# A chunked delta-rule attention with a mixture of attention experts on one core: other PSUM pairs, other scratch, another written order

## The chip, the cores and the metric

One core of one Trainium2 chip runs the whole program, one launch. The metric is device time in microseconds (us) of one execution. Engines: PE (TensorE, matmuls), DVE (VectorE), ACT (ScalarE), POOL (GpSimd), SP (SyncE, which issues most DMAs). Each engine has its own queue and works it off in order.

## The reference

Two parts, one after the other. First, for each of 4 batches and 8 heads, a delta rule over 768 steps with a 48x48 state:

```
k_n = k / (norm(k) + 1e-6)
y[t] = q[t] @ state
state += beta[t] * outer(k_n[t], v[t] - k_n[t] @ state)
```

Then the heads are joined to `x` (4 x 768 x 384), and four experts of width 64 each do causal softmax attention on it:

```
q, k, v = x @ wq[e], x @ wk[e], x @ wv[e]
a = softmax(causal(q @ k.T / 8))
out += gate[e] * (a @ v @ wo[e])
```

The gate is a softmax over the two best of four logits `x @ w_gate`; the others are zero.

## The kernel before, in words

**Tiling.** The sequence is cut into 6 units (`n`) of 4 chunks (`c`) of 64 steps, 2 x 3 units over the batches. Within a chunk the recurrence is a triangular system: `gk` makes k'k products on PE, `ek` brings them to SBUF, `si` transposes 32x32 blocks so that a unit's blocks lie along the free dimension, `pre` gets norms and beta, `pa`, 31 steps `sv` and `pz` invert the triangular blocks by substitution (two tensor-tensor instructions a step, on DVE or POOL by the step's last argument), `so` and `sn` transpose back, and `ma`, eight copies `ea`, `mb`, eight copies `eb` join two 32-blocks to the inverse of 64.

Unit 0 takes another way, which is shorter: `ed` and `en` bring `gk` products to SBUF (`en` the whole masked product), fifteen steps `sb` invert blocks of 16 only, `so.0`/`sn.0` transpose back, and `zx`, `zp`, `ze` double them to 64 by five products a chunk (`zp.c.0` to `zp.c.4`) in four ring buffers for even and four for odd chunks (RING).

**State.** Per chunk: `ks` (k times state), `ex` (v minus it), `uu` (times the inverse), `eu`, `st` and `es` (new state), `yq` and `yu` (outputs, from `gq`/`eq` products and the state), `eh`/`el` (outputs as a high and a low part), and `hx` moves rows by DMA.

**Attention.** Per unit and half: projections `pj` (q and k) and `pv` (v and gate), split to high and low parts by `ph`/`pl`; row maxima `mx`/`em`/`mp`/`mr`/`er`; scores `sc`, exponentials `xp` on ACT, `av`, `oa`, normalising `nm`/`on`, and the output product `ft`, `fh`, `fl`, `fo`, `eo`, `do`. `gates` makes the gate's weights. `lw`, `wh`, `wl` load the weights and split them; `lk`, `lh`, `lv`, `lc`, `lz` load data and constants.

**Order.** Nothing is planned at run time. ORDER is a string of calls, `name.arguments:pair`, and the loop at the end of `tile_kernel` runs it word by word. An engine's queue is the words that issue on it, in that order. The number behind the colon is the PSUM pair (`PP`, 4 pairs of two banks) that the call writes or reads. An argument 0, 1 or 2 at the end of a name is the engine: ACT, DVE, POOL. `fill.n` is n small bf16 products that nothing reads.

In the lines: L182 is every matmul, L186 and L188 the copies of ACT and DVE, L342/L344 `ed`, L348 `en`, L356 `eq`, L360 `si`, L380 to L402 `pre`, L420/L422 `sv`, L425 `zt`, L429 `zm`, L436/L437 `sb`, L452 `sn`, L456 `so`, L302 `wl`, L410 `pz`, L471 `zx`, L619 `pl`, L763 `nm`.

Of the kernel before, what the change touches and what calls it, by code (L numbers as in the profile page):

```python
# [51 lines left out]
sv.1.4.1 eu.0.0.0:2 pre.1.7.1 sv.1.5.2 pre.1.6.1 wl.5.1 fill.3:0 yu.0.0:0 ze.2.0.0:1 zp.3.2:3 sv.1.6.2 eh.0.0.1:0
zp.3.3:3 ze.3.2.0:3 zp.2.1:1 sv.1.7.1 lw.2 ze.3.3.0:3 sv.1.8.2 el.0.0:0 fill.4:2 zp.3.4:2 ze.2.1.0:1 sv.1.9.2 st.0.0:3
lv.0.2 ze.3.4.0:2 gq.0.1:0 lv.0.3 es.0.0:3 gq.0.2:1 sv.1.10.2 wh.2.0 eq.0.1.1:0 wl.2.1 sv.1.11.2 fill.8:2 ks.0.1:2
eq.0.2.1:1 zp.2.2:3 sv.1.12.2 ex.0.1:2 yq.0.1:0 ze.2.2.0:3 uu.0.1:1 lk.2.1 sv.1.13.2 vt.0.2.1 fill.8:2 zp.2.3:3
vt.0.3.2 eu.0.1.0:1 yu.0.1:0 sv.1.14.2 ze.2.3.0:3 st.0.1:2 eh.0.1.0:0 gq.1.0:1 lv.1.0 el.0.1:0 sv.1.15.1 hx.0.0
es.0.1:2 fill.8:3 gq.0.3:3 sv.1.16.2 ks.0.2:0 eq.0.3.1:3 zp.2.4:2 sv.1.17.1 gk.2.0:3 ze.2.4.0:2 vt.1.0.1 sv.1.18.2
ex.0.2:0 eq.1.0.1:1 yq.0.2:2 vo ek.2.0.0:3 sv.1.19.1 gk.2.1:0 lk.2.2 uu.0.2:1 sv.1.20.1 ek.2.1.0:0 sv.1.21.1
pj.0.0.0:3 sv.1.22.1 eu.0.2.1:1 sv.1.23.1 yu.0.2:2 sv.1.24.1 ph.0.0.0.0:3 st.0.2:0 sv.1.25.1 pj.0.0.1:3 lv.1.1
sv.1.26.1 es.0.2:0 sv.1.27.2 eh.0.2.1:2 sv.1.28.2 pl.0.0.0:3 ks.0.3:1 sv.1.29.2 yq.0.3:0 ex.0.3:1 lk.2.3 sv.1.30.1  # L60
uu.0.3:1 vt.1.1.1 sv.1.31.2 eu.0.3.0:1 ph.0.0.1.1:3 st.0.3:1 pl.0.0.1:3 yu.0.3:0 pz.1.2 lv.1.2 es.0.3:1 gk.2.2:3
# [10 lines left out]
es.1.1:2 eg.0.1:0 yq.1.2:1 er.0.0.0:3 mp.0.1.2 sv.2.14.1 sc.0.0.0.0:2 sc.0.0.1.0:0 gates.0.1 xp.0.0.0.0:2 sv.2.15.2
ks.1.2:3 xp.0.0.1.0:0 av.0.0.0.0:2 lk.3.2 ex.1.2:3 sv.2.16.2 gates.0.0 lv.2.0 av.0.0.1.0:0 oa.0.0.0.1:2 mr.0.1:3
oa.0.0.1.0:0 sv.2.17.1 uu.1.2:2 er.0.1.0:3 pj.1.0.0:0 sv.2.18.1 eu.1.2.0:2 gates.0.2 sv.2.19.2 nm.0.0 st.1.2:3
sv.2.20.2 yu.1.2:1 lv.2.1 es.1.2:3 gk.3.2:2 eh.1.2.0:1 ph.1.0.0.1:0 gq.2.1:3 sv.2.21.2 ek.3.2.0:2 pj.1.0.1:0
pl.1.0.0:0 eq.2.1.1:3 on.0.0.2 sv.2.22.1 pv.1.0:3 el.1.2:1 sv.2.23.2 ph.1.0.1.1:0 sv.2.24.2 pl.1.0.1:0 mx.1.1.0.0:2
# [5 lines left out]
fill.8:3 ft.0.1:3 es.1.3:1 eo.0.0.0:2 ma.2:0 pre.3.0.1 fh.0.1.0:3 do.0.0 pj.1.1.0:1 sn.2 pre.3.1.2 vt.2.2.2 fl.0.1:3
pv.1.1:2 ea.2.0.1.1.0:0 ea.2.1.0.1.0:0 ea.2.1.0.0.1:0 ea.2.1.1.1.0:0 pre.3.2.1 ph.1.1.0.0:1 pre.3.3.2 ea.2.0.0.0.0:0
pl.1.1.0:1 pj.1.1.1:1 ea.2.1.1.0.0:0 eg.1.1:2 ea.2.0.0.1.0:0 gates.1.0 pre.3.4.1 ea.2.0.1.0.0:0 gates.1.1 pre.3.5.2
ev.1.1.0:2 pa.3.2 ks.2.0:3 ph.1.1.1.0:1 mb.2:0 ex.2.0:3 pl.1.1.1:1 mx.1.1.1.1:2 eb.2.0.1.1.0:0 eb.2.0.0.0.1:0
mx.1.0.0.1:3 sv.3.1.2 eb.2.0.0.1.0:0 fo.0.1.0:1 em.1.1.1.1:2 eb.2.1.1.0.0:0 sv.3.2.2 eb.2.0.1.0.0:0 eb.2.1.1.1.0:0
pre.3.7.2 eb.2.1.0.0.1:0 yq.2.0:2 eb.2.1.0.1.0:0 sv.3.3.1 uu.2.0:0 lk.4.0 sv.3.4.1 fo.0.1.1:1 eu.2.0.0:0 em.1.0.0.1:3
sv.3.5.2 yu.2.0:2 eo.0.1.0:1 sv.3.6.1 gq.2.3:0 gates.1.2 sv.3.7.2 st.2.0:3 eh.2.0.0:2 do.0.1 mx.1.1.0.1:1 lv.2.3
eq.2.3.0:0 el.2.0:2 es.2.0:3 gk.4.0:2 em.1.1.0.1:1 ks.2.1:3 ek.4.0.0:2 sv.3.8.2 yq.2.1:0 ex.2.1:3 lk.4.1 mx.1.0.1.1:1
uu.2.1:3 sv.3.9.1 sv.3.10.1 sv.3.11.1 eu.2.1.0:3 vt.2.3.2 fill.8:2 yu.2.1:0 em.1.0.1.1:1 st.2.1:2 sv.3.12.2 eh.2.1.0:0  # L90
gq.3.0:3 lv.3.0 lk.5.0 el.2.1:0 gk.4.1:1 eq.3.0.1:3 mp.1.0.2 hx.2.0 es.2.1:2 sv.3.13.2 mr.1.0:0 ks.2.2:3 er.1.0.0:0
mp.1.1.1 ek.4.1.0:1 sc.1.0.0.1:2 sv.3.14.2 ex.2.2:3 fill.2:0 mr.1.1:0 xp.1.0.0.1:2 yq.2.2:1 pre.3.6.1 vt.3.0.1
uu.2.2:3 er.1.1.0:0 lk.4.2 sv.3.15.2 sc.1.0.1.0:2 eu.2.2.1:3 yu.2.2:1 sv.3.16.1 xp.1.0.1.0:2 gq.3.1:0 sv.3.17.2
pj.2.0.0:3 eh.2.2.0:1 eq.3.1.1:0 el.2.2:1 sv.3.18.1 pv.2.0:2 sv.3.19.1 ph.2.0.0.0:3 sv.3.20.1 sv.3.21.1 gk.4.2:0
ev.2.0.0:2 eg.2.0:2 sv.3.22.2 pl.2.0.0:3 mx.2.0.1.0:1 ek.4.2.0:0 mx.2.1.0.0:2 pj.2.0.1:3 em.2.0.1.0:1 sv.3.23.1
em.2.1.0.0:2 sv.3.24.2 av.1.0.1.0:0 ph.2.0.1.0:3 sv.3.25.2 pl.2.0.1:3 mx.2.1.1.0:1 st.2.2:2 em.2.1.1.0:1 sc.1.0.0.0:3
lv.3.1 sv.3.26.2 es.2.2:2 sc.1.1.0.1:1 xp.1.0.0.0:3 sv.3.27.1 ks.2.3:2 sv.3.28.1 xp.1.1.0.1:1 yq.2.3:3 sv.3.29.1
sv.3.30.1 lk.4.3 av.1.0.0.0:1 ex.2.3:2 sv.3.31.2 lv.3.2 av.1.0.0.1:1 vt.3.1.2 pz.3.1 uu.2.3:2 oa.1.0.0.0:1
sc.1.1.0.0:1 eu.2.3.0:2 yu.2.3:3 so.3 xp.1.1.0.0:1 gk.4.3:2 eh.2.3.0:3 av.1.1.0.0:1 ek.4.3.0:2 el.2.3:3 av.1.1.0.1:1
vt.3.2.1 hx.2.1 sc.1.1.1.1:3 sc1.3.0.0 si.4 sc.1.0.1.1:2 xp.1.1.1.1:3 xp.1.0.1.1:2 gq.3.2:3 oa.1.1.0.1:1 pre.4.0.1  # L100
# [780 lines left out]
```

## Time and profile before

| | us |
|---|---|
| median of 3 runs | 451.3 (451.19 to 453.36) |
| profiled execution, its own time | 452.6 |
| its span | 450.9 |
| mean granted PE clock in it | 0.964 |
| PE busy | 392.5 |
| DVE busy | 313.7 |
| ACT busy | 182.0 |
| POOL busy | 171.3 |

The span is from the first to the last instruction of the profiled execution; the 1.7 us around it are start and end of the launch. Busy times are sums over the span, so they average over stages with different limits; a stretch of its own tells more. A wait is put down to what ended it last. [...]

### The profile page before, as it was taken

Reading aid. Unit: us, or ns where it says so; the run is one execution under the profiler, and the core shown is the slowest. Engines: PE = TensorE matmul, PEld = TensorE weight load, DVE = VectorE, ACT = ScalarE, POOL = GpSimd, SP = SyncE. Lnnn points to the kernel's source line nnn. Section 1 sums busy time; section 2 is a strip of 40 time slices with the busy share of each in tenths; the row PEclk is TensorE's granted clock in tenths of the full one; section 3 lists DMA queues with packets and bytes.
Section 4 is the critical chain, followed back from the end, with each engine's and each line's share of the span. In section 5 each row is a group of like instructions: output and inputs, shape, how many; then the busy total and the mean of one; then the engine's idle time right before and its main releaser. Section 6 shows DMA issues by size and latency. Waiting matters only on the chain.

```text
span 450.9 us, 22827 instructions
## 1 busy us (share of the span) xinstructions
PE 392.5 (87%) x10407; PEld 352.6 (78%) x10407; DVE 313.7 (70%) x655; ACT 182.0 (40%) x349; POOL 171.3 (38%) x314
## 2 busy tenths in 40 slices
...
GB/s 187 242 101 17 45 136 85 124 3 75 90 36 45 84 106 124 42 109 20 1 40 132 137 58 1 3 39 40 92 73 82 61 5 10 12 4 38 38 3 70
DMA packets 15441, 29.43 MB, mean 65 GB/s; under 512 B 2801, under 2 KB 8945, under 8 KB 15345
## 3 DMA queue, kind: packets, MB, share of 16 engines
...
q10 hardware_dynamic: 256, 0.39, 0.3%
q14 instruction: 16, 0.12, 0.1%
...
## 4 chain that ended last, share of the span: by engine, by line
PE 67%; DVE 16%; DMA 6%; ACT 5%; issue 4%; POOL 1%; SPq 0%; DVEq 0%; ACTq 0%
PE ps L182 67%; DMA kq<-in_kq_dram 6%; DVE tn L452 2%; ACT tt L186 1%; ACT bl L186 1%; DVE ql L619 1%; DVE xh L590 1%; DVE mx L684 1%; DVE bl L360 1%; DVE tt L190 1%; DVE pm L356 1%; ACT qh L186 1%; DVE tn L436 1%; DVE sb L562 1%; DVE gc L653 1%
## 5 line engine op out<-in xcount | busy, mean ns | idle before, releaser
L422 POOL TENSOR_TENSOR tp<-bl 128x238 f32<-128x238 f32 (+13 forms) x90 | 44.7, 497 | 75.0 <-DVE bl L420 59.2
L743 ACT ACTIVATE at<-ps 128x768 f32<-128x768 f32 (+1 forms) x48 | 43.8, 919 | 40.9 <-PE ps L182 40.7
L182 PE MATMUL ps<-kq 48*64 48x64 f32 x1536 | 38.2, 241 | 16.5 <-issue 5.2
L684 DVE TENSOR_REDUCE mx<-ps 128x2 f32<-128x1024 f32 (+3 forms) x48 | 44.8, 952 | 9.6 <-PE ps L182 9.3
L420 POOL TENSOR_TENSOR bl<-bl,tp 128x238 f32<-128x238 f32 (+13 forms) x90 | 46.6, 518 | 7.1
L182 PEld LDWEIGHTS ps<-kq 48*64 48x64 f32 x1536 | 32.2, 152 | 20.9 <-issue 11.3
L182 PE MATMUL ps<-xh,wqkh 128*128 128x256 f32 x288 | 44.7, 291 | 1.2 <-DVE ql L619 0.9
L182 PE MATMUL ps<-vs,at 128*64 128x65 f32 x1344 | 45.2, 224 | 0.0
L182 PEld LDWEIGHTS ps<-vs,at 128*64 128x64 f32 x1344 | 41.4, 138 | 2.9 <-issue 0.8
L182 PEld LDWEIGHTS ps<-xh,wqkh 128*128 128x128 f32 x288 | 37.9, 191 | 3.1 <-DVE ql L619 1.6
L186 ACT ACTIVATE tt<-ps 32x256 f32<-32x256 f32 (+2 forms) x87 | 33.4, 384 | 15.7 <-PE ps L182 9.6
L182 PE MATMUL ps<-qh,kh 64*128 64x256 f32 x192 | 35.2, 362 | 0.0
L182 PE MATMUL ps<-kh,qh 64*128 64x512 f32 (+3 forms) x128 | 26.3, 435 | 3.6 <-DVE kl L619 1.9
L182 PE MATMUL ps<-ql,kh 64*128 64x256 f32 x192 | 28.1, 289 | 0.0
L182 PE MATMUL ps<-qh,kl 64*128 64x256 f32 x192 | 28.1, 288 | 0.0
L182 PEld LDWEIGHTS <-ide 64*128 64x128 bf16 (+1 forms) x479 | 23.1, 103 | 6.1 <-issue 1.4
L182 PE MATMUL ps<-mr,sel 64*128 64x256 bf16 x192 | 27.4, 281 | 0.0
L182 PE MATMUL ps<-mask,ide 64*128 64x128 bf16 (+1 forms) x384 | 26.1, 217 | 0.0
L182 PE MATMUL ps<-wvgh,xh 128*128 128x260 f32 x144 | 24.8, 297 | 1.4 <-DVE pm L356 1.4
L182 PE MATMUL ps<-xh,wqkl 128*128 128x256 f32 x144 | 24.9, 282 | 0.0
L422 DVE TENSOR_TENSOR tp<-bl 128x210 f32<-128x210 f32 (+14 forms) x60 | 21.4, 357 | 3.0 <-POOL bl L420 2.1
L420 DVE TENSOR_TENSOR bl<-bl,tp 128x210 f32<-128x210 f32 (+14 forms) x60 | 21.6, 360 | 2.1
...
## 6 DMA issues: line engine op xcount, KB each, us to landing
...
kq<-in_kq_dram SPq DMA_DIRECT2D x12, 96.0 KB, 4.2
...
kq<-in_kq_dram ACTq DMA_DIRECT2D x4, 96.0 KB, 3.8
...
```

The costliest lines, as they stand in the source:

```text
L182: T.matmul(o, lhsT=a, rhs=b, start=start, stop=stop, skip_group_check=True)
L186: S.activation(o, x, AF.Copy, **({} if scale is None else {"scale": scale}))
L190: V.tensor_scalar(o, x, scale, None, op0=OP.mult)
L356: (V if e else G).tensor_tensor(t, P if e else t, pmask[:, None, None, :].to_broadcast([128, 2, 4, 64]), op=OP.mult)
L360: V.transpose(BB[n % 2], d.rearrange("p t j -> p j t"))
L420: e.tensor_tensor(X[:, a:b, i + 1:], X[:, a:b, i + 1:], tv, op=OP.subtract)
L422: e.tensor_tensor(tv, R[:, :, i + 1:].to_broadcast([128, w, m]), X[:, a:b, i:i + 1].to_broadcast([128, w, m]), op=OP.mult)
L436: E.tensor_tensor(tv, BD[:, :, i:i + 1, i + 1:].to_broadcast([128, 2, i, m]), BD[:, :, 0:i, i:i + 1].to_broadcast([128, 2, i, m]), op=OP.mult)
L452: V.transpose(TN[n % 2].rearrange("p t l -> p l t"), BB[n % 2])
L562: V.tensor_tensor(s[0:112], s[0:112], ax(k)[0:112], op=OP.add)
L684: V.tensor_reduce(d, two(k)[:, :, a:a + 128 * (k1 - k0)], axis=AX.X, op=OP.max)
L743: S.activation(at_of(n, b, y, kp)[:, :, 0:w], two(k)[:, :, 0:w], AF.Exp, scale=0.125)
```

## The change

Four things. (1) `pj.n.h.0` and `pj.n.h.1`, the q and k projections of a half, wrote the two banks of one pair and now write two different pairs. (2) The ring buffers of odd chunks in unit 0 were `KV[2]`, `PM[1]`, `PM[2]` and `AT[2]`; now they are two parts of `KF` that held `ed`'s result, and two parts of `BX[0]`, the matrix of unit 0's substitution. (3) `en` gets an engine: 1 is the product on DVE out of PSUM as before, 0 a copy on ACT and the product on POOL in place; all four are 0 now. All fifteen `sb` are on DVE (1 to 6 were on POOL). (4) All of ORDER is another: the same calls, each once, in another order, with other engines and pairs, 18 `fill` words (132 products) instead of 16 (95). 55 steps of `sv` go from DVE to POOL and 17 the other way; on POOL are then 133 of 155. Of the 40 `ea` and 40 `eb`, 17 and 15 are on DVE instead of 8 and 10; `on` 8 of 12 instead of 3; `eq` 10 of 24 instead of 16; `eu` 4 of 24 instead of 9; `wl` 1 of 7 instead of 6.

The diff, cut: the start of ORDER, the part around `ma.1` and `mb.1`, and the code.

```diff
-lh.0.1.0.1 zg lc.0 lz lh.0.0.0.0 lh.0.3.0.1 lh.0.2.0.0 lk.1.2 init lk.1.0 lw.0 lc.1 lw.3 lk.1.1 fill.8:0 gk.0.1:0
-ed.1:0 lc.2 gk.0.0:1 lk.1.3 ed.0:1 gk.0.3:2 lv.0.0 ed.3:2 lh.0.3.1.0 gk.0.2:3 ed.2:3 lh.0.1.1.0 lh.0.0.1.0 si.0 lw.1
-lw.5 lh.0.2.1.0 pre.0.0.1 zm lv.0.1 wh.0.0 en.3:2 pre.0.1.2 en.0:1 gk.1.0:2 wh.3.0 pre.0.2.1 gk.1.2:1 ek.1.0.0:2
-pre.0.3.1 wl.3.1 zt pre.0.4.1 cb gk.1.1:2 en.1:0 pre.0.5.2 ek.1.1.0:2 lw.4 pre.0.7.1 gk.1.3:0 ek.1.2.1:1 sb.1.2
-ek.1.3.0:0 sb.2.2 sb.3.2 en.2:3 sb.4.2 si.1 sb.5.2 gq.0.0:2 sb.6.2 lk.2.0 eq.0.0.1:2 wh.1.0 sb.7.1 wh.5.0 sb.8.1
-sb.9.1 sb.10.1 sb.11.1 sb.12.1 sb.13.1 sb.14.1 wh.4.0 sb.15.1 wl.4.2 so.0 sn.0 zx.1.0.0 zx.0.0.0 fill.8:1 zp.1.0:1
-zp.1.1:1 pre.1.0.1 ze.1.0.0:1 zx.1.1.0 zp.0.0:0 pre.1.1.1 wl.1.1 ze.1.1.0:1 zp.0.1:0 pre.0.6.1 ze.0.0.0:0 wl.0.1
...
-eq.1.1.0:2 si.2 yq.1.0:3 sc1.1.0.0 gq.1.2:0 sc1.1.1.0 lk.3.0 pre.2.0.1 eq.1.2.0:0 ma.1:2 ev.0.0.1:1 eg.0.0:1 sn.1
-pj.0.1.0:1 pre.2.1.2 ea.1.0.1.0.1:2 ea.1.1.1.1.0:2 pre.2.2.1 ea.1.1.0.0.0:2 pj.0.1.1:1 pre.2.3.1 ea.1.1.1.0.0:2
-ea.1.0.0.0.0:2 pre.2.6.1 ea.1.0.0.1.0:2 pre.2.4.1 ea.1.0.1.1.0:2 pre.2.5.1 pa.2.1 pre.2.7.2 ea.1.1.0.1.0:2
-ph.0.1.0.0:1 mb.1:2 ph.0.1.1.0:1 pl.0.1.0:1 sv.2.1.2 mx.0.1.1.0:0 eb.1.1.0.1.0:2 eb.1.0.0.0.1:2 sv.2.2.2
-eb.1.0.0.1.0:2 eb.1.1.0.0.1:2 sv.2.3.2 eb.1.0.1.1.0:2 pl.0.1.1:1 eb.1.1.1.0.0:2 eb.1.1.1.1.1:2 eb.1.0.1.0.0:2
...
+lz lc.0 lh.0.3.0.1 fill.22:0 gk.0.3:0 lh.0.1.0.1 lh.0.2.0.0 ed.3:0 fill.1:1 gk.0.1:1 ed.1:1 gk.0.2:2 ed.2:2 lh.0.0.0.0
+gk.0.0:3 ed.0:3 si.0 init lk.1.2 pre.0.0.1 pre.0.1.1 pre.0.2.1 lc.2 lh.0.3.1.0 pre.0.3.1 pre.0.4.1 lw.2 en.1.0:1
+en.2.0:2 zm lh.0.0.1.0 lh.0.2.1.0 pre.0.6.1 lk.1.0 lc.1 pre.0.5.1 en.3.0:0 zt pre.0.7.1 gk.1.2:1 ek.1.2.0:1 cb sb.1.1
+sb.2.1 sb.3.1 gk.1.0:2 lw.0 wh.2.0 lw.3 gq.0.2:1 sb.4.1 sb.5.1 en.0.0:3 eq.0.2.0:1 sb.6.1 lv.0.1 sb.7.1 lh.0.1.1.0
+lk.1.1 sb.8.1 zg wh.3.0 lk.1.3 fill.28:0 gk.1.1:0 wh.0.0 sb.9.1 sb.10.1 sb.11.1 sb.12.1 sb.13.1 sb.14.1 sb.15.1 wl.0.2
+wl.2.2 lw.4 lv.0.2 lw.5 wl.3.2 so.0 fill.5:3 gk.1.3:3 lw.1 lv.0.0 ek.1.0.0:2 ek.1.1.0:0 vt.0.1.2 wh.4.0 ek.1.3.0:3
+gq.0.1:1 eq.0.1.0:1 gq.0.0:2 sn.0 zx.0.0.0 zx.1.0.0 fill.15:0 zp.0.0:0 lw.6 zp.0.1:0 wh.1.0 si.1 pre.1.0.1 zx.0.1.0
+wl.4.2 vt.0.2.2 wh.6.1 ze.0.1.0:0 zp.1.0:3 ze.0.0.0:0 pre.1.1.2 zx.1.1.0 zp.1.1:3 ze.1.1.1:3 wl.6.1 lk.2.0 pre.1.2.1
+pre.1.3.2 zp.0.2:1 wl.1.2 wh.5.0 zp.0.3:1 ze.1.0.0:3 ze.0.3.0:1 ze.0.2.0:1 zp.1.2:0 zp.1.3:0 pre.1.4.1 pre.1.5.2
+zp.0.4:3 eq.0.0.1:2 ze.1.3.0:0 ze.1.2.0:0 ze.0.4.0:3 vt.0.0.2 fill.4:1 uu.0.0:1 zx.2.0.0 eu.0.0.0:1 pa.1.1 pre.1.6.1
...
+ek.2.0.1:3 ev.0.0.1:0 gk.2.3:2 ks.1.0:1 gq.1.2:3 eg.0.0:0 pj.0.0.0:0 pz.1.2 ek.2.3.0:2 eq.1.2.0:3 so.1 si.2 pre.2.0.1
+sc1.1.1.0 sc1.1.0.0 pre.2.1.2 ph.0.0.0.0:0 ex.1.0:1 pl.0.0.0:0 pre.2.2.1 pj.0.0.1:2 ma.1:3 sn.1 vt.1.2.2 pre.2.3.2
+pre.2.4.1 ea.1.0.1.0.1:3 gq.1.1:1 eq.1.1.0:1 pre.2.5.2 ea.1.0.1.1.1:3 pa.2.2 sv.2.1.2 sv.2.2.2 sv.2.3.2 ea.1.1.1.0.1:3
+ea.1.1.0.0.0:3 pre.2.6.1 sv.2.4.2 sv.2.5.2 pv.0.1:0 ea.1.0.0.1.0:3 ph.0.0.1.0:2 pj.0.1.1:1 ea.1.1.0.1.0:3
+ea.1.1.1.1.0:3 ea.1.0.0.0.0:3 ph.0.1.1.0:1 mb.1:3 eg.0.1:0 gates.0.0 sv.2.6.2 sv.2.7.2 eb.1.0.1.1.0:3 pl.0.0.1:2
+sv.2.8.2 sv.2.9.2 ev.0.1.1:0 pre.2.7.1 eb.1.1.0.0.0:3 eb.1.0.0.1.0:3 eb.1.0.1.0.0:3 eb.1.1.1.0.0:3 pj.0.1.0:2
+ph.0.1.0.0:2 eb.1.1.0.1.1:3 eb.1.1.1.1.1:3 yq.1.0:0 eb.1.0.0.0.1:3 pl.0.1.1:1 uu.1.0:3 mx.0.0.0.0:1 lk.3.0 pl.0.1.0:2
...
@@ -343,10 +343,12 @@
         for a in range(2):
             V.scalar_tensor_tensor(d[:, a], P[:, a, :, 0:32], hm[:, 0:1], d[:, a], op0=OP.mult, op1=OP.add)
 
-    def en(c, k):
+    def en(c, e, k):
         P = two(k)[:, :, 0:256].rearrange("p a (b i) -> p a b i", b=4)
-        V.tensor_tensor(TG[0][:, NP * c:NP * c + NP].rearrange("p (a b) i -> p a b i", a=2), P,
-                        nmask[:, None, None, :].to_broadcast([128, 2, 4, 64]), op=OP.mult)
+        t = TG[0][:, NP * c:NP * c + NP].rearrange("p (a b) i -> p a b i", a=2)
+        if not e:
+            S.activation(t, P, AF.Copy)
+        (V if e else G).tensor_tensor(t, P if e else t, nmask[:, None, None, :].to_broadcast([128, 2, 4, 64]), op=OP.mult)
 
     def eq(n, c, e, k):
         P = two(k)[:, :, 0:256].rearrange("p a (b i) -> p a b i", b=4)
@@ -367,7 +369,7 @@
     fl_ = lambda t: t.rearrange("p a b c -> p (a b c)")
     RING = [[x[:, 0:512].rearrange("p (a b) -> p a b", b=64) for x in r] for r in (
         (KF[:, 2432:], fl_(ON), fl_(OS[0]), fl_(OS[1])),
-        (fl_(KV[2]), PM[1].rearrange("p a b -> p (a b)"), PM[2].rearrange("p a b -> p (a b)"), AT[2][:, 0]))]
+        (KF, KF[:, 512:], flat(BX[0]), flat(BX[0])[:, 512:]))]
     BD = BX[0].rearrange("p a b -> p (a b)").rearrange("p (k r) -> p k r", k=2)[:, :, 0:512].rearrange("p k (a b) -> p k a b", b=32)[:, :, :, 0:16]
 
     def pre(n, k, e):
```

## Rows read from the trace of the kernel before

**Rows 1.** Which engine is busy how long, from the page's first part

```profile
PE 392.5 (87%) x10407; PEld 352.6 (78%) x10407; DVE 313.7 (70%) x655; ACT 182.0 (40%) x349; POOL 171.3 (38%) x314
```

**Rows 2.** Stretches: length; PE, PEld, DVE, ACT, POOL busy; PE clock, DMA share, GB/s

```profile
0.00:33.00 33.00, 13.77 (x304) 11.39 (x304) 23.41 (x51) 12.04 (x29) 10.08 (x27) 1.00 0.72 181
...
100.00:373.00 273.00, 249.02 (x6798) 223.08 (x6790) 203.84 (x431) 114.36 (x221) 120.26 (x211) 0.95 0.22 62
373.00:442.00 69.00, 68.24 (x1360) 61.62 (x1360) 31.50 (x65) 25.24 (x34) 6.58 (x18) 0.98 0.07 22
```

**Rows 3.** What PE waited for, 40 to 374 us: total, times, longest

```profile
PE ps L182 <- issue: 12.4, 13, 1.7
PE ps L182 <- DVE kl L619: 2.5, 2, 1.9
...
PE ps L182 <- DVE os L188: 0.4, 1, 0.4
```

**Rows 4.** Busy time by stretch, the six half-rate stretches: first, and sum

```profile
97.70:104.50 6.80, 5.89 (x150) 5.17 (x153) 4.41 (x11) 1.79 (x4) 4.57 (x10) 0.50 0.09 18
...
sum 30.60, PE 29.59 PEld 25.67 DVE 19.04 ACT 7.35 POOL 12.83; mean PE 4.93 PEld 4.28 DVE 3.17 ACT 1.23 POOL 2.14
```

**Rows 5.** Timeline of DVE in the first unit: start, us, line, operation

```profile
18.22 0.67 DVE L400 TENSOR_TENSOR bl<-bl,aa 128x512 f32<-128x512 f32 x1
...
25.50 0.27 DVE L436 TENSOR_TENSOR tn<-bl 128x108 f32<-128x108 f32 x1
...
28.31 0.63 DVE L436 TENSOR_TENSOR tn<-bl 128x28 f32<-128x28 f32 x1
28.98 0.21 DVE L437 TENSOR_TENSOR bl<-bl,tn 128x28 f32<-128x28 f32 x1
...
30.18 1.91 DVE L456 STREAM_TRANSPOSE vs<-bl 128x1024 f32<-128x1024 f32 x1
...
139.97 1.72 DVE L763 TENSOR_TENSOR rsm<-gt,rsm 128x8 f32<-128x8 f32 x1
```

**Rows 6.** Timeline of POOL, the same stretches

```profile
12.54 0.60 POOL L429 MEMSET bl<- 128x256 f32 x2 [9.46 <-DVE bl L360]
...
15.34 1.28 POOL L425 TENSOR_TENSOR bl<-bl,vs 128x512 f32<-128x512 f32 x1 [0.71 <-DVE rr L386]
...
28.09 0.79 POOL L302 TENSOR_TENSOR wvgl<-at,wvgh 128x268 fp32r<-128x268 f32 x1 [4.32 <-ACT wvgh L186]
...
139.76 1.91 POOL L410 TENSOR_TENSOR bl<-bl,na 128x1024 f32<-128x1024 f32 x1
```

**Rows 7.** Timeline of ACT, the start

```profile
2.65 1.28 ACT L284 ACT_TABLE_LOAD   x1 [2.65 <-issue]
...
9.42 0.47 ACT L342 ACTIVATE vs<-ps,cst 128x256 f32<-128x256 f32 x1 [0.38 <-PE ps L182]
...
36.62 0.60 ACT L186 ACTIVATE pm<-ps 128x512 f32<-128x512 f32 x1 [2.80 <-PE ps L182]
```

**Rows 8.** Timeline of PE, the first zp groups and one gq

```profile
33.08 1.97 PE L182 MATMUL ps<-tt,kv 64*64 64x64 f32 x32 [8.47 <-ACT kv L471]
34.84 1.73 PE L182 MATMUL ps<-kv,tt 64*64 64x64 f32 x32
36.41 1.10 PE L182 MATMUL ps<-tt,vs 64*64 64x64 f32 x32
...
64.53 0.69 PE L182 MATMUL ps<-kq 48*64 48x64 f32 x32
```

**Rows 9.** The chain that ended last: start, us, what; one projection half

```profile
359.42 2.41 PE ps L182 x18
```

**Rows 10.** Groups of instructions, one of the two of an sv step

```profile
L422 POOL TENSOR_TENSOR tp<-bl 128x238 f32<-128x238 f32 (+13 forms) x90 | 44.7, 497 | 75.0 <-DVE bl L420 59.2 <-DVE rsm L761 6.1 <-DVE gw L657 5.3
L422 DVE TENSOR_TENSOR tp<-bl 128x210 f32<-128x210 f32 (+14 forms) x60 | 21.4, 357 | 3.0 <-POOL bl L420 2.1
```

**Rows 11.** DMA issues by line, 0 to 60 us: KB each, us to landing

```profile
bta<-in_beta_dram SPq DMA_DIRECT2D x1, 96.0 KB, 7.0
```

More of the change, by code (lines that the diff above doesn't have):

```diff
@@ L52 @@
[L52 to L61, printed above, removed]
@@ L72 @@
[L72 to L76, printed above, removed]
@@ L82 @@
[L82 to L100, printed above, removed]
-mx.2.0.0.0:1 sc1.3.1.0 av.1.0.1.1:0 eq.3.2.1:3 ma.3:2 em.2.0.0.0:1 oa.1.0.1.0:0 sc.1.1.1.0:3 nm.1.0 sn.3 on.1.0.2
```

190 lines of the change are left out of this document (110 added, 80 removed).

## The prediction

> **What bounds the kernel now.** I read the page's totals first. TensorE (PE) is busy 87% of the span, VectorE (DVE) 70%, POOL 38% [rows 1]: PE is the engine to ask about, DVE the one that can hold it. The table of stretches comes next [rows 2]. In the first 33 us PE works 13.8 us, while the DMA engines are 72% busy: that stretch is loading and the first unit's substitution. From 100 to 373 PE works 249.0 of 273 us, and from 373 to 442 it has 68.2 of 69: the last stretch has no stall to win. So an order can win in two places, at the start and in the stalls up to 373.
>
> What ends those stalls is in the table of waits of PE [rows 3]. From 40 to 374 us, 12.4 us in 13 pieces are ended by nothing that the profile shows; the same number of instructions is issued after the change, so I leave them. Twelve lines of DVE, the first 2.5 and the last 0.4, add up to 14.8 us; ACT, POOL and DMA have 5.5. [...]
>
> The sum is made against the profiled execution's own time, 452.6 us (span 450.9 and 1.7 around it), which lies 1.3 above the median of 451.3.
>
> **The start, up to so.0.** `pre.0.7` needs `zt`, which now stands on POOL behind `en.1`, `en.2`, `zm` and `en.3`. The new `en` is a copy on ACT (0.60, by the copy of one PSUM tile at 36.62) and a product on POOL of the size of `zt` (1.28) [rows 6, 7]. `init` and its table load (1.28) now follow the last `ed` on ACT, which ends at 9.89 [rows 7]: the first copy ends at 11.8, and POOL then needs four times 1.28 and 0.6 for `zm` [rows 6], until 17.5. `pre.0.7` (0.67) ends at 18.2; before it ended at 18.89 [rows 5]. Beta is 672 KB later in SP's queue (2699 KB ahead of it instead of 2027). Before it landed 7.0 us behind an issue at about 7.1; at 181 GB/s that is 3.7 us more [rows 2, 11], 17.8, some 0.3 behind `zt`; I take nothing for it, 0.6 if DMA is slower than its mean.
>
> Then all fifteen `sb` run on DVE. Steps 9 to 14 take 3.3 us without the held one (25.50 to 28.31, and twice 0.25); steps 1 to 6 have the same widths, and 7 and 8 cost 0.62 each: 7.8 us. With 0.96 for `sb.15` and 1.91 for `so.0`, `so.0` ends at 28.9 instead of 32.1 [rows 5]: -3.2 at best.
>
> But POOL was nearly idle under DVE's steps, and no longer is. In the one case that overlapped, POOL's `wl.4` ran 28.09 to 28.88 and a DVE step of 0.21 took 0.63, to 28.94; and a DVE product of eight columns took 1.72 until POOL's 1.91 was over [rows 5, 6]. [...] The new order has six POOL operations there (`en.0`, `eq.0.2`, `wl.0`, `wl.2` at 1.28, `wl.3` and `vt.0.1` at 0.79): 6.7 us, less the step of 0.25 that each lets through, +5.2 over the best. The ten operations of `pre` that can be held meet POOL as well: up to 2.5 more. The ends are -3.2 and +4.5; I take +1.0, nearer to the held one, as the rows show it.
>
> [...]
>
> **The start, on PE.** The 32 records of `zp.1.0` and `zp.1.1` took 1.97 and 1.73, the third such group 1.10 [rows 8]: PE came out of idling at the lower level. Now 28, 5 and 15 fills precede `zp.0.0` instead of 8 that ended 8.5 us earlier, so I count 1.97 + 1.73 - 2.2 = -1.5 (0 if PE idles long again). `gq.0.1` and `gq.0.2` move ahead of `zp`, into idle time: two of some 0.5 (32 records in 0.69, the next group beginning before the end) [rows 8], -1.0. The new ring buffers are dead by then, except that `ze.1.0` now writes the matrix that `sn.0` still reads: `sn.0` ends 1.9 behind `so.0`, under three `zp` of 1.1, so nothing; 1.9 if that cover goes.
>
> **Unit 1's entry (ma.1 to uu.1.0).** The longest DVE-ended stall, 1.9 of PE on `kl` [rows 3], is here, followed at once by the first half-rate stretch, 6.8 us [rows 4]. Now `gq.1.1`, `pv.0.1` and `pj.0.1.1` lie behind `ma.1` and `pj.0.1.0` behind `mb.1`: three products of 2.4 [rows 9] where two lay. -1.9 for the stall, and -1.7 for half of the 3.4 that the clock can give back: -3.6 (0 to -5.3).
>
> **DVE against POOL from there on.** 38 steps of `sv` go from DVE to POOL, two instructions each, 0.36 on DVE and 0.50 on POOL [rows 10]: 27 us less on DVE, 38 more on POOL. Five `on` (0.7) and 14 copies of `ea` and `eb` (0.4) come to DVE, 9 us, and `en`, `eq`, `eu` and `wl` leave it for about as much: it falls to some 290 us. All of it lies beside PE's work; it pays only where a DVE line ends a stall. Of the 14.8 less the 1.9 above I take -1.0 (0 to -12.9): a new order also makes new stalls.
>
> **A pair for each projection.** A projection takes 2.41 [rows 9]; two halves held one pair, now each has its own until its copies are done. Nothing shows four pairs under such use. PE's waits for `kl`, 2.5 [rows 3], can go, or as much can come where another matmul waits for a pair: -2.5 to +2.5, and I take 0, since the 1.9 is counted already.
>
> **Fills.** 95 become 132, but behind `zp.0.0` and before the last eight groups 63 become 45. Eight warm ones are some 0.8: 18 fewer are at most -1.8; most stood in stalls, so -0.5.
>
> Sum: +1.0 - 1.5 - 1.0 - 3.6 - 1.0 + 0 - 0.5 = -6.6. 452.6 becomes 446.0, and on the median's scale 444.7: I say **445 us**. About 0.5% is what a measurement here can tell from no change: under 449.0 counts as faster, over 453.6 as slower.
>
> **Rivals.**
> *POOL holds DVE (slower).* [...] Price: +4.5 instead of +1.0 at the start; unit 1's chain is then late, so 3.6 and the 1.0 of relief are not gained, and holds in later `gates` and `nm` add some 1.5: 445 + 3.5 + 3.6 + 1.0 + 1.5 = 455. It decides from `so.0` ending after about 36. For it: the held rows. [...]
> *Stalls move (same).* PE stays bound by its queue, and each stall that goes returns elsewhere. Only the start's terms remain, -1.5: 450.
> *The clock stays up (faster).* The stalls that precede half-rate stretches go. [...] For it: PE's cover is better at unit 1. Against it: five of the six stretches lie where I see no edit aimed at them.
> [...]
> *The change doesn't do what it says* would be projections whose halves still wait for each other; it prices as the second rival.
>
> **Chances.** Forecast 0.48 (own range 440 to 449), stalls move 0.20, POOL holds DVE 0.20, clock 0.12. Faster than 449.0: nearly all of the first and last, a few of the second, 0.60; same 0.20; slower 0.20. The range reaches half way into the clock case and just over the hold: 437 to 456.
>
> **What would show it.** In the changed profile: `so.0` ending near 33 (29 without holds, over 36 with all), and `sb` steps beside POOL operations longer than 0.3; the first `zp` at 1.1; no stall of over 1 us before `uu.1.0` and the clock whole from 97 to 105; DVE's busy time near 290 and POOL's near 215; PE's DVE-ended waits under 13 us. The prediction is wrong if `zp.0.0` starts after 38, or if half-rate time exceeds 31 us.

## The result, and the profile after

| | median us | lowest to highest | runs |
|---|---|---|---|
| before | 452.27 | 446.16 to 457.24 | 20 |
| after | 446.23 | 442.36 to 449.58 | 20 |

The ratio is 0.990, with a 95% interval of 0.9865 to 0.9928: the kernel after is 1.0% faster. The prediction was 445 us, 1.4% under the 451.3 known then. The profiled execution of after took 449.6 us (span 447.9), the highest of its 20 and one of four in a slower state, which the ratio leaves out, so the two traces differ by only 3.0 us where the medians differ by 6.0. The trace of e5, the same kernel once more at 446.9 us (span 445.2), is set beside it where that matters.

The page's first part, against [rows 1]:

```profile
PE 391.5 (87%) x10444; PEld 356.2 (80%) x10444; DVE 301.2 (67%) x598; ACT 180.8 (40%) x344; POOL 219.8 (49%) x381
```

DVE lost 12.5 us and POOL gained 48.5; PE is as busy as it was. The stretches, with the columns of [rows 2]:

```profile
0.00:33.00 33.00, 18.40 (x423) 15.87 (x423) 24.12 (x50) 14.61 (x35) 17.97 (x22) 0.80 0.79 206
100.00:373.00 273.00, 248.48 (x6968) 225.36 (x6972) 195.32 (x381) 116.64 (x223) 163.30 (x290) 0.95 0.22 63
```

In the first 33 us POOL works 18.0 us instead of 10.1. What that did to DVE stands in two timelines of after, DVE first, then POOL (start, us, line, operation; L438 and L439 are the two instructions of a step `sb`, lines being two higher than before; a POOL row of x2 is two operations in a row):

```profile
22.21 0.25 DVE L438 TENSOR_TENSOR tn<-bl 128x88 f32<-128x88 f32 x1
22.49 1.20 DVE L439 TENSOR_TENSOR bl<-bl,tn 128x88 f32<-128x88 f32 x1
23.72 1.23 DVE L438 TENSOR_TENSOR tn<-bl 128x100 f32<-128x100 f32 x1
...
27.07 1.21 DVE L439 TENSOR_TENSOR bl<-bl,tn 128x108 f32<-128x108 f32 x1
28.32 0.72 DVE L438 TENSOR_TENSOR tn<-bl 128x112 f32<-128x112 f32 x1
29.08 0.78 DVE L439 TENSOR_TENSOR bl<-bl,tn 128x112 f32<-128x112 f32 x1
29.89 0.27 DVE L438 TENSOR_TENSOR tn<-bl 128x112 f32<-128x112 f32 x1
...
34.75 1.91 DVE L458 STREAM_TRANSPOSE vs<-bl 128x1024 f32<-128x1024 f32 x1
```

```profile
22.21 2.62 POOL L302 TENSOR_TENSOR wqkl<-at,wqkh 128x512 fp32r<-128x512 f32 x2
24.79 1.31 POOL L302 TENSOR_TENSOR wvgl<-at,wvgh 128x512 fp32r<-128x512 f32 x1
26.05 0.86 POOL L531 TENSOR_TENSOR kv<-kv,nt 128x384 f32<-128x384 f32 x1
26.88 1.28 POOL L358 TENSOR_TENSOR pm<-pm,cst 128x512 f32<-128x512 f32 x1
28.12 0.79 POOL L302 TENSOR_TENSOR wvgl<-at,wvgh 128x268 fp32r<-128x268 f32 x1
28.88 0.85 POOL L531 TENSOR_TENSOR kv<-kv,nt 128x384 f32<-128x384 f32 x1
```

Seven POOL operations stand back to back from 22.21 to 29.73, and seven DVE instructions each end some 0.1 us behind one of them: DVE got one instruction in for each of POOL's. While POOL is idle the same DVE instruction takes 0.27. `so.0` ends at 36.66; before it was 32.09 [rows 5].

PE's waits over the whole span (line, what ended the wait: us, times, longest):

```profile
PE ps L182 <- ACT vs L473: 11.3, 1, 11.3
PE ps L182 <- issue: 6.1, 7, 2.4
...
PE ps L182 <- POOL bl L422: 5.5, 2, 3.5
...
PE ps L182 <- DVE kl L621: 1.0, 2, 0.8
```

The waits that "issue" ends have halved from [rows 3]'s 12.4, and those on `kl` fell from 2.5 to 1.0. The 11.3 is PE waiting for `zx` at the start. Added up by engine, before to after: issue 12.4 to 6.1, DVE 21.8 to 16.2, ACT 13.7 to 17.1, DMA 4.1 to 5.7, POOL 0.8 to 5.8; together 52.9 to 50.9 us. So what two kinds of waits lost, the others took back, all but 1.9 us. Of DVE's 5.6, 4.8 is one wait on `en` at the start; from 40 to 374 us DVE's go from 14.8 to 13.9 only. (The 5.5 under POOL is really ACT's: it lies before `mb.1` and `mb.2`, and ACT's last copy `ea` ended 0.1 us before each began.) In e5's trace the waits are 52.0 us, 0.9 less than before's, and PE's busy time is 387.7 instead of 392.5: of the 5.7 us by which its span is shorter, 4.8 are busy time. Clock and first `zp`, from the timeline of PE and the stretches at half rate, against [rows 4, 8]:

```profile
37.75 1.97 PE L182 MATMUL ps<-tt,vs 64*64 64x64 f32 x32 [11.32 <-ACT vs L473]
39.48 1.94 PE L182 MATMUL ps<-vs,tt 64*64 64x64 f32 x32
```

```profile
sum 36.45, PE 34.95 PEld 32.98 DVE 19.45 ACT 12.96 POOL 25.59; mean PE 4.99 PEld 4.71 DVE 2.78 ACT 1.85 POOL 3.66
```

PE came to `zp.0.0` after 11.3 us of idling, and the clock granted from 37.75 to 43.6 was 0.51; from 37.75 to 307 us seven stretches, 36.5 us in all, ran at half rate (a granted 0.50, in the first 0.51), where before had 30.6. Between these two traces the clock gained nothing; in e5's the same stretches from `zp.0.0` on add up to 28.6. (The sum is that of a row by stretch, as in [rows 4]. Before's profile gives 1.00 from 33 to 36 us although its first `zp` groups took 1.97 and 1.73 there, so its 30.6 may lack some 3 us, and the clock of the first 33 us can't be compared.)

### The profile page after: what moved, and what is told of

The parts are those of the page before. It is cut to its first block, busy times and chain, and to the rows that moved or that the text cites. A ratio compares the mean times of both kernels' runs of the same rounds, so it can differ in the third digit from the quotient of the medians.

```text
span 447.9 us, 22876 instructions
## 1 busy us (share of the span) xinstructions
PE 391.5 (87%) x10444; PEld 356.2 (80%) x10444; DVE 301.2 (67%) x598; ACT 180.8 (40%) x344; POOL 219.8 (49%) x381
## 3 DMA queue, kind: packets, MB, share of 16 engines
q1 hardware_dynamic: 15088, 27.59, 21.8%
## 4 chain that ended last, share of the span: by engine, by line
PE 54%; DVE 23%; POOL 11%; issue 5%; ACT 4%; DMA 2%; ACTq 0%; DVEq 0%; POOLq 0%
PE ps L182 54%; POOL bl L422 3%; POOL tp L424 3%; DVE mx L686 2%; DVE bl L362 2%; DMA kq<-in_kq_dram 2%; POOL bl L408 2%; DVE bl L439 2%; DVE xh L592 1%; DVE tn L438 1%; DVE tt L458 1%; DVE tp L424 1%; ACT tt L186 1%; POOL kv L531 1%; DVE sb L564 1%
## 5 line engine op out<-in xcount | busy, mean ns | idle before, releaser
L424 POOL TENSOR_TENSOR tp<-bl 128x84 f32<-128x84 f32 (+13 forms) x128 | 63.6, 497 | 29.8 <-DVE bl L422 19.0
L422 POOL TENSOR_TENSOR bl<-bl,tp 128x84 f32<-128x84 f32 (+13 forms) x128 | 67.7, 529 | 10.0
L182 PE MATMUL ps<-vs,at 128*64 128x65 f32 x1344 | 43.6, 223 | 0.0
L182 PE MATMUL ps<-kq 48*64 48x64 f32 x1536 | 34.4, 229 | 9.8 <-DMA kq<-in_kq_dram 5.7
L182 PEld LDWEIGHTS ps<-vs,at 128*64 128x64 f32 x1344 | 40.8, 138 | 2.2 <-issue 0.9
L186 ACT ACTIVATE tt<-ps 32x256 f32<-32x256 f32 (+2 forms) x83 | 32.1, 386 | 22.3 <-PE ps L182 19.4
L358 POOL TENSOR_TENSOR pm<-pm,cst 128x512 f32<-128x512 f32 x14 | 18.0, 1283 | 45.1 <-ACT pm L357 45.0
L182 PEld LDWEIGHTS ps<-kq 48*64 48x64 f32 x1536 | 29.0, 141 | 13.7 <-issue 6.4
L182 PEld LDWEIGHTS <-ide 64*128 64x128 bf16 (+1 forms) x516 | 26.9, 100 | 6.8 <-issue 1.9
L182 PE MATMUL ps<-kh,qh 64*128 64x512 f32 (+3 forms) x128 | 24.9, 415 | 1.3 <-DVE kl L621 1.0
L186 ACT ACTIVATE ub<-ps 128x384 f32<-128x384 f32 x20 | 9.8, 490 | 35.6 <-PE ps L182 28.2
```

The costliest lines, as they stand in the source:

```text
L182: T.matmul(o, lhsT=a, rhs=b, start=start, stop=stop, skip_group_check=True)
L186: S.activation(o, x, AF.Copy, **({} if scale is None else {"scale": scale}))
L358: (V if e else G).tensor_tensor(t, P if e else t, pmask[:, None, None, :].to_broadcast([128, 2, 4, 64]), op=OP.mult)
L422: e.tensor_tensor(X[:, a:b, i + 1:], X[:, a:b, i + 1:], tv, op=OP.subtract)
L424: e.tensor_tensor(tv, R[:, :, i + 1:].to_broadcast([128, w, m]), X[:, a:b, i:i + 1].to_broadcast([128, w, m]), op=OP.mult)
```

## The experiments

Each ratio is against before, run beside it on the same chip. In the first four experiments before had a median of 456.1, in e5 to e8 453.4, in e9 to e12 454.6. A projection's two halves, below, are its q and its k part, `pj.n.h.0` and `pj.n.h.1`; there are twelve such pairs of halves. Lines of the runs' kernels are some higher or lower than those of before.

| run | median us | ratio to before, 95% interval |
|---|---|---|
| e1_hold | 441.9 | 0.971 [0.966, 0.976] |
| e2_sv_engines | 507.1 | 1.113 [1.108, 1.118] |
| e3_head_after | 465.3 | 1.020 [1.014, 1.025] |
| e4_head_before | 469.8 | 1.028 [1.023, 1.033] |
| e5_after_again | 445.8 | 0.985 [0.980, 0.990] |
| e6_one_pair | 467.4 | 1.029 [1.023, 1.035] |
| e7_before_sv | 458.3 | 1.009 [1.005, 1.014] |
| e8_start | 441.9 | 0.976 [0.971, 0.980] |
| e9_before_apart | 451.6 | 0.994 [0.989, 0.998] |
| e10_hold_again | 440.6 | 0.971 [0.966, 0.975] |
| e11_start_again | 440.0 | 0.970 [0.965, 0.974] |
| e12_warm | 446.4 | 0.984 [0.979, 0.989] |

### Is it POOL that holds DVE, and does the start reach the end?

**e1_hold.**

```
+    def hold():
+        G.tensor_copy(hd, BB[0][:, 31, 31:32])
...
-sb.14.1 sb.15.1 wl.0.2 wl.2.2
+sb.14.1 sb.15.1 hold wl.0.2 wl.2.2
```

> The kernel after, with one 1-column copy on POOL that reads the result of sb.15, put ahead of wl.0: POOL's wl.0, wl.2, wl.3, vt.0.1, eq.0.1, wl.4 and vt.0.2 can't start before DVE's fifteen sb are over. If those POOL operations are what stretched sb.4 to sb.7 (eight steps of 0.7 to 1.2 us that each ended with one of them), the steps fall back to about 0.27, and so.0 ends near 31 us instead of 36.7. Then, theory 1 (the start's slip reaches the end): the time falls by 4 to 5 us, to about 442, ratio to before 0.978. Theory 2 (the slip is taken up by PE's queue behind it, or the seven operations hold DVE as much where they now run): within 1.5 us of the kernel after, ratio 0.987 to 0.993. If so.0 does not move, the hold by POOL is not the cause.

**e5_after_again** (no edit) and **e10_hold_again** (the same edit again):

> The kernel after, unchanged, beside the runs of before on this chip: the yardstick for the three others of this call and for the hold. Theory 1 (the 5 us that the hold took off the start reached the end): this one lies 4 to 6 us above e1_hold's 441.9, with a ratio near 0.990. Theory 2 (that chip's runs of before were high): its ratio here is as low as the hold's 0.971.

> e1_hold once more, as the yardstick on this chip for the next two, and to see whether its ratio to before holds: 0.966 to 0.976 if e1 told the truth, near 0.985 if the hold is worth nothing.

DVE in e1_hold, the same steps on the same engine, with POOL waiting:

```profile
22.76 0.25 DVE L437 TENSOR_TENSOR bl<-bl,tn 128x88 f32<-128x88 f32 x1
23.04 0.26 DVE L436 TENSOR_TENSOR tn<-bl 128x100 f32<-128x100 f32 x1
...
29.72 1.96 DVE L460 STREAM_TRANSPOSE vs<-bl 128x1024 f32<-128x1024 f32 x1
```

The order changed in this one word alone, and 1.20 became 0.25 (it is seven stretched instructions, not eight). `so.0` ended at 31.68, 5.0 us earlier than in after. The time fell as theory 1 said, or by more: 441.9 and 440.6 on two chips against 446.2 and 445.8 for after, and ratios of 0.971 and 0.971 against 0.990 and 0.985. A copy of one column took 4 to 6 us off the kernel by the medians and 6 to 9 by the ratios (e5 and the hold ran on different chips), and PE's waits added up are 44.5 and 44.6 us in its two traces instead of 50.9 and 52.0: the 5.0 us of the start go into the total at least nearly one for one.

### Is it DVE's relief, or the engines of the steps?

**e2_sv_engines** and **e7_before_sv**, such words for 72 of the 155 steps, in opposite directions:

```
e2, on after:   -sv.3.3.2   +sv.3.3.1
e7, on before:  -sv.3.3.1   +sv.3.3.2
```

> The kernel after, in its own order, but each step of sv in units 1 to 5 on the engine that it had before (55 steps back from POOL to DVE, 17 from DVE to POOL, 38 net). DVE's busy time rises by about 27 us to some 328, POOL's falls by about 38 to some 182. Theory 1 (DVE's relief is what paid): most of the 5 to 6 us that the kernel after has gained goes, time about 450 to 455, and DVE-ended waits of PE rise from 16 us to 20 or more. Theory 2 (the order paid, not who does the steps): time 445 to 448, as the kernel after.

> The kernel before, in its own order, with the steps of sv on the engines that after has them on (55 to POOL, 17 to DVE). In before the chain of sv steps stands 40.8 us in 31 gaps where a step on POOL is followed by one on DVE, which takes its turn in DVE's queue; after has 4.4 us in 10 such gaps, and longer POOL steps. Theory 1 (these hand-overs are what paid): gaps of that kind fall under 10 us, and the time is 444 to 449, as after. Theory 2 (order and engines only fit together, as the 12% of e2 suggest): 453 or more.

e2 was far outside both expectations: 507 us. e7 was slower than before by 0.9%, as its theory 2 had it. The first part of the pages of e2 and of e7:

```profile
PE 417.3 (83%) x10444; PEld 377.6 (75%) x10444; DVE 320.3 (63%) x674; ACT 181.4 (36%) x344; POOL 180.3 (36%) x305
```

```profile
PE 394.6 (86%) x10407; PEld 354.4 (78%) x10407; DVE 287.0 (63%) x579; ACT 181.9 (40%) x349; POOL 208.9 (46%) x390
```

e7 is the relief by itself. DVE's busy time falls by 26.7 us against [rows 1], POOL's rises by 37.6, as the prediction counted them, and nothing is gained. The gaps in which a DVE step waits its turn behind POOL's do fall, from 40.8 us to 5.6, but the chain of steps from `sv.n.1` to `sv.n.30`, added up over five units, stays: 204.8 us before, 207.3 in e7. POOL's longer steps (11 us more) and the gaps between two steps on POOL, where its other work lies (7.0 to 34.8 us), take their place. In after the chain is 199.5, in e2 250.2: there the steps stand in DVE's queue at places where other words of the new order come first, and the steps themselves are not longer. PE's waits in e2, 40 to 440 us, show who is late for it:

```profile
PE ps L180 <- DVE xb L538: 15.3, 6, 4.3
PE ps L180 <- DVE ql L619: 6.8, 2, 5.9
```

In before's order, then, moving the steps gains nothing and costs 0.9%. That after's relief helps it inside its own order can't be told from this; it is only shown that the order can't do without it.

### Can the loss at the front be parted from the gain behind it?

**e3_head_after** and **e4_head_before**:

```
e3: words of after up to st.1.0, then what is left, in before's order
e4: words of before up to st.1.0, then what is left, in after's order
```

> The kernel after up to uu.1.0 and st.1.0 (its first 106 us), then everything that is left in the order, on the engines and, but for 5 values, in the pairs of before. Theory 1 (the new order lost 7 us up to there and won about 10 behind it, each by itself): 106.6 us and the 351.7 that before took from there on, 460 in all, slower than before by 6 to 8 us. Theory 2 (what the later part wins is work that the slower head had moved ahead or made ready): 446 to 453.

> The other half of it: before up to uu.1.0 and st.1.0 (its first 99 us, with its scratch buffers and its substitution), then everything that is left in the order and on the engines of after; 15 values sit in another pair than after has them in. Theory 1 (losses and gains lie apart): 99.2 us and the 341.3 that after took from there on, 442 in all, faster than both kernels. Theory 2 (the later gain needs the new head): 448 to 453.

e3 came out at theory 1's price: its ratio of 1.020 is 461 us on the scale of before's 452.3, where 460 was expected. Its `uu.1.0` began at 109.9 us (the same words took 106.6 in after; why, stays open), and the rest took 353.5, before's 351.7 within half a per cent. e4 was to be the gain without the loss, 442, and is 469.8, which neither theory had: `uu.1.0` at 102.1, and then 365.9 us for what took after 341.3. So the front does cost what it seems to, and theory 1 stops there: after's later order is no better by itself. Behind another front, which leaves the queues and the pairs in another state, it loses 25 us; e4 also had to put 15 values into other pairs, and how much of the 25 that is, no run parts.

### What is a pair for each half worth?

**e6_one_pair** on after, **e9_before_apart** on before:

```
e6, on after:   -pj.0.0.1:2  +pj.0.0.1:0     (pj.0.0.0 in pair 0)
e9, on before:  the halves of eleven projections to two pairs, such as 0 and 3
```

> The kernel after, with both halves of a projection in one PSUM pair for eleven of the twelve projections (the twelfth, of unit 3, has its halves too far apart), as before has it; 57 words change their pair for it, the order and the engines stay. Theory 1 (the halves in pairs of their own let PE go on): slower than the kernel after by 1 to 2.5 us, with waits of PE that an el, ph or pl ends in the projections. Theory 2 (0, as predicted: the halves lie in different banks and do not wait for each other): within 1 us of e5_after_again.

> The kernel before, order and engines unchanged, with the two halves of eleven of its twelve projections in pairs of their own (46 words change their pair). Theory 1 (the pair by itself pays: in e6 the second half waited up to 4.3 us for the copies of the first): the waits of PE on kl and ql, 2.5 us in before, go, and the time is 2 to 4 us lower, ratio 0.991 to 0.996. Theory 2 (before's order has other work between the halves and needs its free pairs elsewhere; the pair pays only with an order made for it): ratio 0.997 to 1.01.

e6 shows the mechanism, and a price ten times theory 1's. PE and then DVE around the second half of the first projection:

```profile
89.14 0.52 PE L180 MATMUL ps<-xh,wqkl 128*128 128x256 f32 x3
93.94 0.39 PE L180 MATMUL ps<-xh,wqkh 128*128 128x256 f32 x1 [4.27 <-DVE ql L619]
```

```profile
87.97 2.29 DVE L456 STREAM_TRANSPOSE tt<-bl 128x1024 f32<-128x1024 f32 x1 [1.39 <-POOL bl L411]
90.15 1.90 DVE L360 STREAM_TRANSPOSE bl<-tt 128x1024 f32<-128x1024 f32 x1
...
93.20 0.68 DVE L619 TENSOR_TENSOR ql<-ps,qh 128x512 fp32r<-128x512 f32 x1
```

The first half's products end at 89.7; their second copy, `pl.0.0.0`, stands in DVE's queue behind two transpositions and four small operations and ends at 93.9; only then does the second half begin, although it writes another bank of the pair. In the program a pair is one tile (`PP`), and by the profile the matmul waits for a semaphore that the copy sets. The sum of PE's waits, 40 to 450 us:

```profile
PE ps L180 <- DVE ql L619: 7.7, 2, 4.3
PE ps L180 <- DVE kl L619: 6.1, 5, 1.9
```

That is 13.8 us of waits, 12.7 of them in five pieces ahead of a second half; e5's trace has 0.9 of waits on `kl` and `ql` in all. The time is 21.6 us above e5's on the same chip (16.0 between the two profiled executions). 24 of the 57 words are others that had to make room, so the price is that of all of them.

In e9 the same freedom, given to before's order, is worth 0.65% [0.2, 1.1], some 3 us: theory 1's time, though the interval reaches into theory 2's. The sign that theory 1 named did not come. The waits on `kl` and `ql`, 3.4 us in before, are 4.7 here:

```profile
PE ps L179 <- DVE kl L616: 4.5, 4, 1.7
```

What went are other waits: between `uu.5.0` and `uu.5.3` PE idles 1.2 us where it idled 4.2 in before, and the waits of the whole span are 49.6 instead of 52.9. 13 of e9's 46 words are not of projections either, so that the 3 us are the halves' is not shown. A reason why sharing costs so much more in after stands in the two orders: a second half can wait for the copies of the first only where these come ahead of it, and both copies do so in eight of after's twelve projections and in four of before's.

### The rest of the start

**e8_start**, **e11_start_again** and **e12_warm**, on e1_hold:

```
e8:  -en.1.0:1 en.2.0:2 zm ... en.3.0:0 zt    +si.0 en.1.0:1 en.2.0:2 zm zt
e8, e11:  en.0, en.3, eq.0.2 parted: copy on ACT in place, POOL's product behind hold
e12: -fill.15:0   +fill.60:0
```

> e1_hold, and the rest of the hold by POOL taken out of the start: zm and zt follow en.2 on POOL at once, and POOL's products of en.0, en.3 and eq.0.2 are parted from their copies on ACT and stand behind the hold. Four DVE operations of pre.0 that took 0.8 to 1.2 us beside POOL's would fall to about 0.2, and so.0 end 2.5 to 3 us earlier than in e1_hold, near 28.8. Theory 1 (the start's chain reaches the end one for one): 439 to 440. Theory 2 (from here PE, cold, or the loads set the pace): 441 to 443.

> e8_start with zm and zt back in their old place, behind the steps of pre.0 that read the diagonal; POOL's products of en.0, en.3 and eq.0.2 stay behind the hold. The first tensor_scalar of pre.0, and the product after it, are no longer held; zt itself still holds two steps. so.0 ends 1.5 to 3 us before e10_hold_again's, near 29.5. Theory 1 (the start passes to the end): 1.5 to 3 us below e10_hold_again. Theory 2 (PE, cold when zp.0.0 starts, sets the pace from there): within 1 us of it.

> e11_start_again with 60 fills instead of 15 ahead of zp.0.0, so that PE works up to the moment when zx.0.0 is done, instead of idling some 4 to 5 us. Theory 1 (the clock counts here): zp.0.0 to zp.1.1 take 1.1 us each instead of 1.95, half-rate time up to uu.1.0 falls by 5 us or more, and the time is 2 to 4 us below e11_start_again. Theory 2 (DVE's and ACT's copies pace these products, or the clock falls behind them in any case): within 1 us, the granted clock whole at zp.0.0 or not.

In e8 `zt` multiplies the diagonal by zero ahead of the norms that read it, so only its time is read. DVE and then POOL in e11:

```profile
16.36 1.15 DVE L407 TENSOR_SCALAR nn<-g 128x32 f32<-128x32 f32 x1
17.54 0.19 DVE L408 TENSOR_TENSOR rr<-nn 128x32 f32<-128x32 f32 x1
...
18.45 0.69 DVE L416 TENSOR_TENSOR bl<-bl,aa 128x512 f32<-128x512 f32 x1
19.18 0.19 DVE L452 TENSOR_TENSOR tn<-bl 128x28 f32<-128x28 f32 x1
```

```profile
16.18 1.28 POOL L441 TENSOR_TENSOR bl<-bl,vs 128x512 f32<-128x512 f32 x1 [2.03 <-DVE rr L402]
17.52 1.93 POOL L309 MEMSET tt<- 32x1024 f32 x2
```

Beside a product on POOL (16.18 to 17.46) a 32-column DVE operation with one input took 1.15, to 17.51; beside a memset, 1.93 for the two, none of the four two-input operations was held: they took 0.19, 0.19, 0.69 and 0.19 (the third took 0.67 in before [rows 5] and 1.58 in after, where a product ran beside it). But in e8 a one-input operation that takes 0.18 in e11 took 0.97 beside a memset, and in after one took 0.92, to 12.83, where a memset ended at 12.78. What parts these two from the four no run shows. `so.0` ended at 29.83 in e11, 1.4 us before e10's, and the time is the same: 440.0 and 440.6. Theory 2: here the pace has gone over to the products and copies behind `zx`. e8, whose `so.0` ended at 30.36 instead of the 28.8 expected, came out at theory 2's price, 441.9, and adds nothing to that. e12 shows what the clock is worth at this place (granted 1.00 from 31.1 to 34.8 us, in e11 0.50 from 30.9 to 33.9), PE in e12 and then in e11:

```profile
25.70 5.12 PE L180 MATMUL ps<-ide 128*128 128x192 bf16 x60
31.07 1.15 PE L180 MATMUL ps<-tt,vs 64*64 64x64 f32 x32 [0.25 <-ACT vs L491]
...
37.94 1.15 PE L180 MATMUL ps<-bl 64*64 64x64 f32 x32 [1.03 <-ACT bl L184]
```

```profile
30.91 1.98 PE L180 MATMUL ps<-tt,vs 64*64 64x64 f32 x32 [2.80 <-ACT vs L491]
32.64 1.69 PE L180 MATMUL ps<-vs,tt 64*64 64x64 f32 x32
...
37.88 1.11 PE L180 MATMUL ps<-bl 64*64 64x64 f32 x32
```

The fills worked: 1.15 instead of 1.98 and 1.69. But then PE waits 1.03 for a copy on ACT, and by `zp.1.2` the two kernels are level: nothing gained, as theory 2 said. What neither theory said is that e12 is 6.4 us slower than e11. Its trace is 3.5 us longer than e11's; the waits that "issue" ends grew by 6.0 (e11 first), all others fell by 3.9, and PE is busy 1.4 longer:

```profile
PE ps L180 <- issue: 4.8, 7, 1.3
PE ps L180 <- issue: 10.8, 12, 2.2
```

Why 45 more fills at 30 us should bring such waits at 58 to 335 us is taken up at the end; that they are the 6.4 us is not shown.

## Why the prediction came out right, point by point

The time was inside the range, near the value, and faster as forecast. Most of the steps that led there were wrong, and errors of both signs cancelled: that the value was met so closely is luck.

**What bounds the kernel**: right in that PE's stalls and the start are what an order can win. Wrong in "12.4 us in 13 pieces are ended by nothing that the profile shows; the same number of instructions is issued after the change, so I leave them". They fell to 6.1, the largest single change in the table of PE's waits, and e5's trace has 6.2 again: it belongs to the kernel, not to the execution. (Nor is the number the same: the 37 more fills make 10444 matmuls of 10407. The 14.8 us of DVE's lines stand in thirteen lines, not twelve.) In the experiments PE's waits, added up over the span, do go with the time: 52.9 in before, 44.5 with the hold, 49.6 in e9, 56.6 in e7, 67.6 in e6, 83.3 in e2. For the change itself they hardly move.

**The start, up to so.0**, +1.0 with ends of -3.2 and +4.5: it was +4.6, at the far end. The row that showed a hold (0.63 for 0.21 [rows 5]) was read rightly and then weighed half. The far end's own terms came out: the seven held instructions are 5.3 us longer than without a hold, for 5.2, and `pre` ended 2.5 later than its 18.2, at 20.7, for "up to 2.5 more". Which operations they are came out otherwise: `en.0` and `eq.0.2` ran under `pre`, and since DVE was late, `eq.0.1`, `wl.4` and `vt.0.2` came to lie under the steps. e1 shows cause and price: 5.0 us at `so.0`, at least 4 to 6 at the end. That ten operations of `pre` can be held, from which the 2.5 came, no run shows: in after five of them took 0.92 to 1.58 us.

**The start, on PE**, -1.5 for `zp` at full clock: not obtained. The first three groups took 1.97, 1.94 and 1.94 (1.97, 1.95 and 1.68 in e5), slower than before's 1.97, 1.73 and 1.10. The 28, 5 and 15 fills ended long before, because `so.0` was late; and in e12, behind the hold, even a `zp` at a granted 1.00 gained nothing. For `gq.0.1` and `gq.0.2`, -1.0, no run parts them from the rest.

**Unit 1's entry**, -3.6: not obtained. From the end of `so.0` to the start of `uu.1.0` before took 67.1 us and after 69.9. The stall on `kl` did go, and so did the half-rate stretch behind it (none from 75 to 159 us), as the prediction's signs had it. But `mb.1` now waits 1.9 for a copy `ea`, two waits on `xb` add up to 2.0, and the first `zp` groups and 3.4 us at 71 run at half rate; part of the difference is `pv.0.1`, which has moved ahead of `uu.1.0`.

**DVE against POOL**, -1.0: POOL's busy time was right (215, in fact 220), DVE's fell by half of what was forecast (to 301, not some 290; held instructions count as busy, and with the hold it is 296.6 and 293.5), and the gain was not in them. e7 moves the same 27 us and loses 0.9%. DVE-ended waits did not fall under 13 us.

**A pair for each projection**, 0 between -2.5 and +2.5: mis-sized. The edit that gives the halves pairs of their own is worth some 3 us in before's order (e9), and the new order rests on them with up to 21.6 us (e6). "Nothing shows four pairs under such use" was true of the trace; the two orders show it, by where the copies stand between two halves.

**Rivals.** *POOL holds DVE* was half right. Its point of decision was passed (36.66, "after around 36"), its price at the start was paid in full, and unit 1's 3.6 was lost, as it said; the total did not follow, because the gain lies elsewhere: from `uu.1.0` on, after is 10 us shorter. *Stalls move* describes PE's waits best: 52.9 us of them became 50.9, and 52.0 in e5, at other places. Its time of 450 is out, since the interval on the scale of 451.3 is 445.2 to 448.1. *Doesn't do what it says* is out, by e6. *The clock stays up* is not seen: half-rate time from `zp.0.0` on was 36.5 us in the one trace, past the mark of 31 that was to make the prediction wrong, and 28.6 in e5's. What a clock that stays up would be worth, the 437 at which the range begins, no run shows; in e12 the first `zp` groups ran at a granted 1.00, and its time was 446.4 for e11's 440.0.

**Where the gain is** stays open. Shown: some 3 us for the edit of the pairs in before's own order (e9); the new front loses, and the hold takes back at least 4 to 6 (e1); neither the engines of `sv` (e7) nor the later order behind another front (e4) gains anything by itself. No run changes the ring buffers alone, or the engines of `ea`, `eb`, `on`, `eq`, `eu` and `wl`. In the traces the largest single term is the 6.3 us of "issue" waits, but the other waits take it back, and such waits don't order the times: e10's trace has 7.8 us of them at 439.6, e11's 4.8 at 441.9. What is shorter in e5's trace is PE's busy time, by 4.8 us, and that differs by 5.6 between two traces of one kernel (e1 and e10). One pair of traces can't place a change of this size.

The version that beats both is after with the hold: 0.971 [0.966, 0.975]; with `en.0`, `en.3` and `eq.0.2` parted as well it is 0.970 [0.965, 0.974], no different.
